# Linear sums over a whole group in 32-row tiles, paired 64-row transposes of x, no clip in the gate, and another written order

## The chip, the cores and the metric

The kernel runs on one core of a Trainium2 chip. The metric is the device time of one execution in microseconds, as the median of several runs. Before the change three runs took 248.51, 249.53 and 250.40 us, so the median is 249.53 us.

## What is computed

There are 4 batches of 12,480 rows x of width 128, and 32 inducing rows. Two attention steps follow one another, and a gated feed-forward layer stands behind them:

```python
def mab(q, kv):
    s = scale * (q @ kv.transpose(0, 2, 1))
    s = s - s.max(-1, keepdims=True)
    a = np.exp(s)
    a /= a.sum(-1, keepdims=True) + 1e-09
    return a @ kv
h = mab(I, x)          # 32 rows a batch
y = mab(x, h)          # 12480 rows a batch
g = y @ w_in                                   # 128 -> 2048
out = (g * np.clip(g + 3.0, 0.0, 6.0) / 6.0) @ w_out   # 2048 -> 128
```

Each row of y is a weighted mean of the 32 rows of h. While |g| stays below 3 the gate is the polynomial g(g+3)/6, so an output row is a linear sum over the 32 weights plus a quadratic sum over pairs of weights. The kernel computes h for a batch, multiplies its 32 rows through w_in, and folds w_out into two small matrices: one for the linear sums and one (four blocks of 128 pairs) for the quadratic sums. A test at the end counts entries that would leave the range of the approximation and branches to a plain version if there are any.

## The kernel before, in words

**Tiling.** A batch is cut into six groups of 2,048 rows and one of 192. Within a full group, partition p holds 16 consecutive rows. For the second attention these are seen as 4 slots s by 4 lanes j (J = 4, Sn = 4); a half h of a group is two slots.

**First attention, per group.** `op_X` loads x through GpSimd's queue, cast to fp16 on the way, into one of 7 buffers. `op_T` (line 422) transposes 8 or 16 blocks of 128x128 on TensorE into PSUM, `op_Y` (line 428) copies eight of them to xT. `op_S` forms scores, `op_E` the exponentials, `op_A` the sums over rows of x and `op_H` adds them to a batch's accumulator.

**Once a batch.** `op_c3` to `op_cN` turn the accumulator into the small matrices: `op_G` is the product with w_in, `op_cH` (line 543, GpSimd) and `op_cI` (line 548, VectorE) make g * min(max(g+3, 0), 6) from it, `op_L` multiplies by w_out, `op_cN` (line 595) writes the linear matrix BD, and `op_p`, `op_P`, `op_cX`, `op_cY` make the quadratic matrix Cq. `op_cJ` (line 553, VectorE) keeps the largest |g| for the test at the end. BD is written with a mask, so that each of its 64-row halves is a block-diagonal matrix for two lanes.

**Second attention and output, per group.** `op_Z` makes two score forms in PSUM; ScalarE and VectorE turn them into z, e, dk; `op_W` spreads dk over partitions with a DMA of 128 KB issued by SyncE's queue. For each half, `op_B` (line 731) repeats z over pairs into four PSUM banks and `op_F` (line 741, ScalarE, two instructions a half) takes the exponential into TF; `op_U` (line 750, VectorE) multiplies by the spread dk into TD. The sums are taken in PSUM: `op_l` (line 770) adds the linear part from ee and BD, `op_q` (line 789) the quadratic part from TF (u = 0) and TD (u = 1) with Cq. `op_v` multiplies a finished bank by the row's factor and writes it to os (line 807 on VectorE, line 811 on ScalarE in four pieces), and `op_O` stores os to memory from SyncE's queue.

A bank of the output sums holds one half h and one pair of lanes jp: two slots by two lanes by 128 columns. It gets two linear matmuls of 64 rows by 256 columns and 16 quadratic ones of 128 columns. A half needs two such banks; a full group uses four, two at a time or as the order has it.

**Order.** There is no scheduler. The string `ORDER` lists about 1,400 tokens such as `q.0.2.1.0.1.5`; each is one `op_` call, with batch, group, half and so on, the numbers of its PSUM banks (0 to 7) and, where there is a choice, the engine (V, A or P). Every engine executes its own instructions in the order of the string, and semaphores make an instruction wait for what it reads and for the buffer or bank that it overwrites. `op_w` issues matmuls on zeros, which only keep TensorE going while the first loads are under way.

Of the kernel before, what the change touches and what calls it, by code (L numbers as in the profile page):

```python
# [32 lines left out]
cD.0.0.V T.1.0.8.16.0 T.1.0.0.8.4 X.1.3.0.16 cH.0.P cD.0.1.A Y.1.0.8.16.0.V S.1.1.0.16.6 Y.1.0.0.8.4.A W.0.0.3
E.1.1.0.16.6 Z.0.3.0.5 Z.0.2.0.7 cI.0 Zz.0.2.7 p.0.2.V W.0.2.3 B.0.0.0.2.0 S.1.0.0.16.4 F.0.0.0.0.2 E.1.0.0.16.4 L.0.0.6
A.1.1.0.16.7 W.0.2.0 H.1.1.0.16.7 L.0.1.6 cL.0.6 p.0.1.V A.1.0.0.16.4 cM.0.0.6 W.0.1.0 Ze.0.0 cm.0.3 ee.0.0.V cN.0.3
cM.0.1.7 F.0.0.0.1.0 Ze.0.1 cC.0 wb.1.P T.1.3.8.16.2 H.1.0.0.16.4 R.0.0.0 wb.0.P Y.1.3.8.16.2.A p.0.3.V T.1.3.0.8.1
wb.2.P Rr.0.0.0 wb.3.P P.0.1.6 P.0.2.7 p.0.0.V Y.1.3.0.8.1.A R.0.1.4 Rr.0.1.4 R2.0.1.V X.1.2.0.16 B.0.0.1.2.0 Zz.0.3.5
F.0.0.1.1.0 P.0.3.7 F.0.0.1.0.2 cP.0.1.7 P.0.0.6 cP.0.0.6 W.0.1.3 W.0.1.2 B.0.1.0.4.0 F.0.1.0.0.4 Z.0.3.1.7 Zd.0.3.7
U.0.0.1 cX.0.0.3 S.1.3.0.16.2 cY.0.0.3.A F.0.1.0.1.0 T.1.2.8.16.6 T.1.2.0.8.4 Y.1.2.8.16.6.V E.1.3.0.16.2 cX.0.1.5
q.0.0.1.1.0.7 Ze.0.3 cY.0.1.5.V Y.1.2.0.8.4.V q.0.0.0.1.0.6 l.0.0.0.0.6 W.0.1.1 l.0.0.1.1.7 B.0.1.1.2.4 R2.0.0.V  # L40
q.0.0.0.0.0.0 q.0.0.1.1.1.7 U.0.0.0 q.0.0.0.0.1.0 v.0.0.1.1.7.V W.0.3.2 F.0.1.1.1.4 F.0.1.1.0.2 v.0.0.0.0.0.V
q.0.0.0.1.1.6 v.0.0.0.1.6.V q.0.0.1.0.0.1 q.0.0.1.0.1.1 B.0.2.0.2.4 R.0.3.0 v.0.0.1.0.1.V Ze.0.2 R.0.2.6 Rr.0.3.0
S.1.2.0.16.7 W.0.2.1 W.0.2.2 X.1.4.0.16 W.0.3.1 T.1.4.0.8.1 Rr.0.2.6 Y.1.4.0.8.1.V F.0.2.0.0.2 A.1.3.0.16.0 Z.0.4.1.6
W.0.3.0 X.1.5.0.16 X.2.4.0.16 W.0.3.3 Z.0.5.1.2 F.0.2.0.1.4 H.1.3.0.16.0 Z.0.4.0.3 Zd.0.4.6 E.1.2.0.16.7 B.0.2.1.0.4
# [986 lines left out]
```

## Time and profile before

| what | value |
|---|---|
| median of three runs | 249.53 us |
| the profiled execution, its own time | 249.51 us |
| its span, first to last instruction | 247.5 us |
| what lies outside the span | 2.0 us |
| TensorE busy, weight loads busy | 92%, 75% |
| VectorE, ScalarE, GpSimd busy | 82%, 77%, 16% |
| mean granted TensorE clock | 0.982 |

The profile's page gives the busy time of each engine, the same in 40 equal slices of the span, and groups of instructions by line. PE is TensorE's matmuls, PEld its weight loads, DVE is VectorE, ACT ScalarE, POOL GpSimd, SP SyncE. Matmuls are pipelined: one of 128 columns is listed at some 220 ns, while the next begins 56 ns after it. What a step takes is therefore read from where the next one starts in the timeline, not from its listed length. An idle time is given with what ended it. Times inside the program are counted from the start of the span.

### The profile page before, as it was taken

How to read it: one execution, taken by the hardware profiler on the slowest of the kernel's cores; microseconds unless marked ns; L12 is line 12 of the kernel's file. 1: busy time of each engine (PE TensorE's matmuls, PEld its weight loads, DVE VectorE, ACT ScalarE, POOL GpSimd, SP SyncE). 2: the span in 40 equal slices, each digit the busy share in tenths (PEclk: the TensorE clock that was granted, in tenths of full speed). 3: DMA queues.
4: the chain of work that ended last, by engine and by line, in shares of the span. 5: the costliest groups of instructions: out<-in, count | busy, mean ns of one | idle time of the engine just before them, and what ended most of it. 6: DMA issues, size and time to landing. Idle time of an engine off the chain costs nothing. (4 is left out here: it accounts for less than half of the span.)

```text
span 247.5 us, 10076 instructions
## 1 busy us (share of the span) xinstructions
PE 227.0 (92%) x4317; PEld 186.5 (75%) x4317; DVE 202.4 (82%) x438; ACT 191.1 (77%) x350; POOL 40.3 (16%) x80
## 2 busy tenths in 40 slices
PE   1879799999799999999899999999999999989990
PEld 0568758888698798797787888888878877768780
DVE  0236879989599997999778998988889999998983
ACT  2167277998788886999687786999889889989870
POOL 8518582021002500010004000000031000000000
PEclk9999679999999999999999999999999999999998
DMA  6999789969989999849879974623981849696953
GB/s 96 193 255 254 238 158 193 208 163 250 214 286 263 277 196 331 293 87 250 184 252 265 266 274 110 224 56 76 338 305 37 262 97 340 211 311 170 362 232 134
DMA packets 23744, 53.91 MB, mean 218 GB/s; under 512 B 3697, under 2 KB 16785, under 8 KB 20753
## 3 DMA queue, kind: packets, MB, share of 16 engines
q1 hardware_dynamic: 19072, 38.36, 47.4%
q0 software_dynamic: 4624, 14.88, 31.0%
q8 instruction: 34, 0.56, 0.8%
q14 instruction: 14, 0.11, 0.1%
HBM read 27.67 MB, written 25.56 MB: 215 GB/s over the span
## 5 line engine op out<-in xcount | busy, mean ns | idle before, releaser
L741 ACT ACTIVATE TF<-ps 128x1024 f16<-128x1024 f32 (+1 forms) x100 | 96.8, 1007 | 16.1 <-PE ps L731 12.4
L750 DVE TENSOR_TENSOR TD<-TF,d 128x2048 f16<-128x2048 f16 (+1 forms) x52 | 59.9, 1156 | 3.0 <-ACT TF L741 2.2
L789 PE MATMUL ps<-Cq,TF 128*128 128x128 f16 (+1 forms) x784 | 57.9, 219 | 2.6 <-issue 1.4
L789 PE MATMUL ps<-Cq,TD 128*128 128x128 f16 (+1 forms) x784 | 56.0, 219 | 0.0
L807 DVE TENSOR_TENSOR os<-ps,r 128x512 f32<-128x512 f32 x68 | 45.4, 683 | 11.7 <-PE ps L789 4.1
L789 PEld LDWEIGHTS <-TF 128*128 128x128 f16 (+1 forms) x784 | 46.3, 98 | 6.3 <-issue 6.0
L789 PEld LDWEIGHTS <-TD 128*128 128x128 f16 (+1 forms) x784 | 46.1, 99 | 4.3 <-issue 3.4
L811 ACT ACTIVATE os<-ps,r 128x128 f32<-128x128 f32 x112 | 32.0, 380 | 4.3 <-PE ps L789 2.0
L422 PE MATMUL ps<-ident_h,xh 128*128 128x128 f16 x384 | 29.8, 226 | 5.5 <-DMA xh<-in_x_dram 5.5
L422 PEld LDWEIGHTS <-xh 128*128 128x128 f16 x384 | 24.0, 102 | 11.6 <-DMA xh<-in_x_dram 7.5
L428 DVE COPY xT<-ps 128x1024 f16<-128x1024 f16 x31 | 21.2, 684 | 12.8 <-PE ps L422 12.5
L428 ACT COPY xT<-ps 128x1024 f16<-128x1024 f16 x17 | 17.0, 1015 | 18.9 <-PE ps L422 18.8
L416 POOL DMA_DIRECT2D xh<-in_x_dram x25 | 13.9, 560 | 75.1 <-PE ps L459 62.2
L731 PE MATMUL ps<-z,pair 32*128 32x256 f16 (+1 forms) x400 | 20.3, 270 | 0.0
L609 DVE TENSOR_TENSOR PR<-Gd 128x2048 bf16<-128x2048 bf16 x16 | 19.8, 1239 | 0.0
L678 DVE TENSOR_SCALAR_CACHE_REDUCE z<-ps 128x512 f16<-128x512 f32 (+1 forms) x28 | 17.3, 621 | 2.4 <-PE ps L656 2.3
L666 ACT ACTIVATE dk<-ps 128x512 f16<-128x512 f32 (+1 forms) x28 | 14.8, 547 | 5.5 <-PE ps L656 3.4
L770 PE MATMUL ps<-BD,ee 64*128 64x256 f16 (+1 forms) x196 | 17.5, 273 | 0.2
L441 ACT ACTIVATE a<-ps 128x512 f16<-128x512 f32 (+1 forms) x27 | 14.6, 556 | 2.6 <-PE ps L433 2.6
L616 PE MATMUL ps<-w_ob,PR 128*128 128x128 bf16 x256 | 16.5, 219 | 0.0
L671 ACT ACTIVATE e<-z 128x512 f16<-128x512 f16 (+1 forms) x28 | 16.3, 589 | 0.1
L616 PEld LDWEIGHTS <-PR 128*128 128x128 bf16 x256 | 14.7, 98 | 0.9 <-issue 0.8
(137 smaller groups left out, 284.8 us busy)
## 6 DMA issues: line engine op xcount, KB each, us to landing
out_dram<-os SPq DMA_DIRECT2D x23, 1024.0 KB, 5.2
d<-dk SPq DMA_DIRECT2D x96, 128.0 KB, 3.9
xh<-in_x_dram POOLq DMA_DIRECT2D x23, 512.0 KB, 8.8
os<-in_moe_w_in_dram POOLq DMA_DIRECT2D x2, 512.0 KB, 13.4
w_or<-in_moe_w_out_dram POOLq DMA_DIRECT2D x2, 512.0 KB, 11.6
out_dram<-os SPq DMA_DIRECT2D x2, 512.0 KB, 3.6
xh<-in_x_dram POOLq DMA_DIRECT2D x2, 256.0 KB, 7.3
out_dram<-osl SPq DMA_DIRECT2D x4, 96.0 KB, 3.0
```

What stands on the lines that cost most here:

```text
L422: nc.tensor.transpose(pt[:, (i - lo) * p : (i - lo + 1) * p], at(xh, xhl, b, g)[:p, i, :], ident_h[:p, :p])
L428: copier(e)(xT_of(b, g)[:, lo * p : hi * p], ps[:, k, :].bitcast(FP16)[:, : (hi - lo) * p])
L609: veng(e).tensor_mul(pr_of(b, c)[:, :, :].rearrange("p a (i m) -> p a i m", m=M), views[0], views[1])
L616: nc.tensor.matmul(ps[:, k, f * C : (f + 1) * C], lhsT=pr_of(b, c)[:, jb, :], rhs=w_ob[:, jb, :], start=first_of(b, u), stop=False, skip_g ...
L678: nc.vector.tensor_scalar(fat(z_, b, g)[:rows, :w], ps[:rows, k, :w], 1.0, None, op0=ALU.mult, op1=ALU.min, accum_out=z_all[:rows, b * NGR ...
L731: nc.tensor.matmul(ps[:, pairs[j // 2] + j % 2, f * w : (f + 1) * w], lhsT=pair[rows, f, :], rhs=fat(z_, b, g)[rows, h * w : (h + 1) * w], ...
L741: nc.scalar.activation(hat(TF_, b, g, h)[:, 2 * q : 2 * q + 2, :w], ps[:, k : k + 2, :w], ACT.Exp, scale=scale / KH)
L750: nc.vector.tensor_mul(split(hat(TD_, b, g, h)), split(hat(TF_, b, g, h)), d.unsqueeze(2).to_broadcast([P, J, 2, w]),)
L770: nc.tensor.matmul(ps[:p, ks[jp], s2 * 2 * C : (s2 + 1) * 2 * C], lhsT=fat(e2_, b, g)[rows, s * p : (s + 1) * p], rhs=BD_[b % 2][rows, :, ...
L789: nc.tensor.matmul(ps[:p, k, (s2 * 2 + j2) * C : (s2 * 2 + j2 + 1) * C], lhsT=t[:, j, f * w + s2 * p : f * w + (s2 + 1) * p], rhs=Cq_[b % ...
L807: nc.vector.tensor_mul(o, src, r.unsqueeze(3).to_broadcast([p, Sh, 2, C]))
L811: nc.scalar.mul(o[:, s2, j2, :], src[:, s2, j2, :], r[:, s2, j2 : j2 + 1])
```

## The change

- **Linear sums.** An output bank now holds one lane j with all four slots of a group (both halves). `op_l` runs once a group and issues 16 matmuls of 32 rows by 128 columns, four row tiles side by side, each into its own bank. BD is a plain 128x128 copy; the mask is gone. A bank gets 4 linear and 16 quadratic matmuls as before in number, but its quadratic ones come from both halves, so a group opens four banks together and `op_v` can empty one only behind the second half.
- **Transposes.** For batches 1 to 3, `op_TT` transposes a full group in 32 matmuls of 64 rows by 64 columns: two row tiles, one into each of two banks, for each of 16 blocks. `op_YY` copies one such bank to xT in 64-column pieces. x comes in two halves, X.b.g.0.8 and X.b.g.8.16, 36 loads in place of 18. Batch 0 and the groups of 192 rows keep `op_T` and `op_Y`, and batch 0 now loads group 0 whole as well.
- **No clip.** `op_cH` is gone; `op_cI` computes (g+3)*g at once. The test takes the sum of squares of g on ScalarE (`op_cJ`) against 9 in place of the largest |g| on VectorE against 3.
- **Stores.** `op_O` can store two lanes of a group; the last group is stored so.
- **Order.** All of ORDER is new. With it go these counts of instructions: `op_v` 74 on VectorE and 22 calls (88 pieces) on ScalarE, before 68 and 28 calls (112 pieces); copies to xT of 1,024 columns 23 on VectorE and 25 on ScalarE, before 31 and 17; matmuls on zeros 24, before 16; w_hi copies 1 on VectorE and 3 on ScalarE, before 3 and 1; w_lo 3 on VectorE, before 2; w_ob three of four on ScalarE, before all on GpSimd; the Gd copies 5 of 8 on ScalarE, before 4.

```diff
-it X.0.1.0.16 i2 i1 w.2.0 i3.V T.0.1.0.8.1 Y.0.1.0.8.1.V i0 w.2.5 w.2.2 X.0.0.8.16 T.0.0.8.16.1 w.2.7 Y.0.0.8.16.1.V
+i0 i2 w.2.4 w.2.2 w.2.7 wi.1 w.2.0 X.0.0.0.16 w.2.2 w.2.3 i1 i8 X.0.6.0.2 w.2.0 i3.V T.0.0.0.8.1 it Y.0.0.0.8.1.V
...
-        BD_ = ring("BD", 2, [P, 2, C], FP16)
+        BD_ = ring("BD", 2, [P, C], FP16)
...
+        def op_TT(b, g, *ks):
+            for i in range(TG):
+                for r in range(2):
+                    rows = slice(64 * r, 64 * r + 64)
+                    nc.tensor.transpose(
+                        ps[:, ks[r], :].bitcast(FP16)[:, i * 64 : (i + 1) * 64],
+                        at(xh, xhl, b, g)[rows, i, :],
+                        ident_h[rows, rows],
+                        tile_position=(64 * r, 0),
+                    )
+
+        def op_YY(b, g, r, k, e):
+            copier(e)(
+                xT_of(b, g)[:, :].rearrange("c (i r t) -> c r i t", r=2, t=64)[:, r],
+                ps[:, k, :].bitcast(FP16).rearrange("c (i t) -> c i t", t=64),
+            )
...
-        def op_cH(b, e):
-            veng(e).tensor_scalar(
-                r6[:, :, :], GL[:, :, :M].bitcast(FP32), 3.0, 0.0, op0=ALU.add, op1=ALU.max
-            )
-
         def op_cI(b):
             nc.vector.scalar_tensor_tensor(
-                GL[:, :, M:], r6[:, :, :], 6.0, GL[:, :, :M].bitcast(FP32), op0=ALU.min, op1=ALU.mult
+                GL[:, :, M:],
+                GL[:, :, :M].bitcast(FP32),
+                3.0,
+                GL[:, :, :M].bitcast(FP32),
+                op0=ALU.add,
+                op1=ALU.mult,
             )
 
         def op_cJ(b):
-            nc.vector.tensor_reduce(
-                g_all[:, b : b + 1],
+            nc.scalar.activation(
+                junk[:, :].rearrange("p (a m) -> p a m", m=M),
                 GL[:, :, :M].bitcast(FP32),
-                axis=AX.XY,
-                op=ALU.max,
-                apply_absolute_value=True,
+                ACT.Square,
+                accum_out=g_all[:, b : b + 1],
             )
...
-        def op_l(b, g, h, *ks):
-            t0, p, J, Sn = groups[g]
-            Sh = (Sn + 1) // 2
-            for s2 in range(Sh):
-                s = h * Sh + s2
-                for jp in range(J // 2):
-                    rows = slice(64 * jp, 64 * jp + 64)
+        def op_l(b, g, *ks):
+            t0, p, J, Sn = groups[g]
+            for s in range(Sn):
+                for j in range(J):
+                    rows = slice(32 * j, 32 * j + 32)
                     nc.tensor.matmul(
-                        ps[:p, ks[jp], s2 * 2 * C : (s2 + 1) * 2 * C],
+                        ps[:p, ks[0] + j if g == NG else ks[j], s * C : (s + 1) * C],
                         lhsT=fat(e2_, b, g)[rows, s * p : (s + 1) * p],
-                        rhs=BD_[b % 2][rows, :, :].rearrange("p j c -> p (j c)"),
+                        rhs=BD_[b % 2][rows, :],
-                        tile_position=(64 * jp, 0),
+                        tile_position=(32 * j, 0),
                     )
...
-                            ps[:p, k, (s2 * 2 + j2) * C : (s2 * 2 + j2 + 1) * C],
+                            ps[:p, ks[0] + j2 if g == NG else ks[j2], (h * Sh + s2) * C : (h * Sh + s2 + 1) * C],
```

**How the order moves, on VectorE near the end of batch 3.** The rows are instructions of VectorE in their order, with no time in them. TD<-TF,d is `op_U` of one half, os<-ps,r is `op_v`, r<-rc is the factor of a group, rc<-ps its reciprocal, ee<-e the square of e. Before, around the fourth and fifth groups of the batch:

```order
L717 RECIPROCAL rc_163<-ps 128x16
L807 TENSOR_TENSOR os_118<-ps,r_165 128x2x256
L723 TENSOR_TENSOR r_165<-rc_163 128x16
L692 TENSOR_TENSOR ee_100<-e_97 64x96
L723 TENSOR_TENSOR r_165<-rc_164 128x16
L750 TENSOR_TENSOR TD_115<-TF_112,d_110 128x2048
L807 TENSOR_TENSOR os_117<-ps,r_165 128x2x256
L750 TENSOR_TENSOR TD_116<-TF_113,d_111 128x2048
L807 TENSOR_TENSOR os_117<-ps,r_165 128x2x256 x3
L750 TENSOR_TENSOR TD_115<-TF_114,d_111 128x2048
```

The same place now:

```order
L812 TENSOR_TENSOR os_118<-ps,r_163 128x4x128 x4
L725 RECIPROCAL rc_161<-ps 128x16
L758 TENSOR_TENSOR TD_116<-TF_114,d_110 128x2048
L731 TENSOR_TENSOR r_163<-rc_162 128x16
L758 TENSOR_TENSOR TD_115<-TF_112,d_110 128x2048
L758 TENSOR_TENSOR TD_116<-TF_113,d_111 128x2048
L812 TENSOR_TENSOR os_117<-ps,r_163 128x4x128
L686 TENSOR_SCALAR z_103,z_all<-ps 64x96
L812 TENSOR_TENSOR os_117<-ps,r_163 128x4x128 x2
L758 TENSOR_TENSOR TD_115<-TF_114,d_111 128x2048
```

Before, a bank is emptied between the two products of a group; now both products (TF_114 and TF_112 with d_110) stand ahead of the first bank of that group (os_117).

**And at VectorE's end.** junk,cnt rows are the counts of the test; tot is the copy of their sum. Before:

```order
L807 TENSOR_TENSOR os_118<-ps,r_165 128x2x256 x2
L717 RECIPROCAL rc_164<-ps 96x2
L723 TENSOR_TENSOR r_165<-rc_164 96x2
L831 TENSOR_SCALAR junk,cnt<-g_all 128x4
L831 TENSOR_SCALAR junk,cnt<-d_all 128x128 x2
L831 TENSOR_SCALAR junk,cnt<-c_all 128x4 x2
L831 TENSOR_SCALAR junk,cnt<-h_all 128x4
L831 TENSOR_SCALAR junk,cnt<-z_all 128x28
L831 TENSOR_SCALAR junk,cnt<-r_165 128x98
L858 COPY tot<-ps 1x9
```

Now:

```order
L839 TENSOR_SCALAR junk,cnt<-z_all 128x28
L812 TENSOR_TENSOR os_118<-ps,r_163 128x4x128
L731 TENSOR_TENSOR r_163<-rc_162 96x2
L758 TENSOR_TENSOR TD_116<-TF_112,d_109 128x2x192
L812 TENSOR_TENSOR os_118<-ps,r_163 128x4x128
L812 TENSOR_TENSOR osl_120<-ps,r_163 96x256
L839 TENSOR_SCALAR junk,cnt<-r_163 128x98
L839 TENSOR_SCALAR junk,cnt<-r_163 128x294
L839 TENSOR_SCALAR junk,cnt<-g_all 128x4
L839 TENSOR_SCALAR junk,cnt<-d_all 128x128 x2
L839 TENSOR_SCALAR junk,cnt<-c_all 128x4 x2
L839 TENSOR_SCALAR junk,cnt<-h_all 128x4
L866 COPY tot<-ps 1x9
```

The count of z moved ahead of the last products, the count of 294 factors moved to the end, and the last output bank (osl) now stands on VectorE ahead of the counts.

More of the change, by code (lines that the diff above doesn't have):

```diff
@@ L153 @@
+O.3.6.0.2 y1 O.3.5.8.16 y0 y3 y4.3 y5.3
 """
@@ L351, in op_i6 @@
                 e.memset(blk[rows, j : j + 1], math.sqrt(KC))
-                e.memset(mask[rows, j % 2, :], 1.0)
             e.memset(fac[:, :], KC / 3.0)
@@ L594, in op_cN @@
         def op_cN(b, k):
[L595 to L597 removed]
+            nc.vector.tensor_copy(BD_[b % 2][:, :], ps[:, k, :C])
         def pr_of(b, c):
@@ L796, in op_q, with op_v @@
                         )
-        def op_v(b, g, h, jp, k, e):
+        def op_v(b, g, j, k, e):
             t0, p, J, Sn = groups[g]
-            Sh = (Sn + 1) // 2
-            o = at(os_, osl, b, g)[:p, : J * Sn, :].rearrange("p (s j) c -> p s j c", j=J)
-            o = o[:, h * Sh : (h + 1) * Sh, 2 * jp : 2 * jp + 2, :]
-            src = ps[:p, k, : Sh * 2 * C].rearrange("p (s j c) -> p s j c", j=2, c=C)
-            r = r2_of(b, g, 0, J * Sn).rearrange("p (s j) -> p s j", j=J)
-            r = r[:, h * Sh : (h + 1) * Sh, 2 * jp : 2 * jp + 2]
+            js = slice(0, J) if g == NG else slice(j, j + 1)
+            o = at(os_, osl, b, g)[:p, : J * Sn, :].rearrange("p (s j) c -> p j s c", j=J)[:, js]
+            src = ps[:p, k : k + js.stop - js.start, : Sn * C].rearrange("p j (s c) -> p j s c", c=C)
+            r = r2_of(b, g, 0, J * Sn).rearrange("p (s j) -> p j s", j=J)[:, js]
             if e == "V":
-                nc.vector.tensor_mul(o, src, r.unsqueeze(3).to_broadcast([p, Sh, 2, C]))
-            else:
-                for s2 in range(Sh):
-                    for j2 in range(2):
-                        nc.scalar.mul(o[:, s2, j2, :], src[:, s2, j2, :], r[:, s2, j2 : j2 + 1])
+                n = js.stop - js.start
+                nc.vector.tensor_mul(o, src, r.unsqueeze(3).to_broadcast([p, n, Sn, C]))
+            else:
+                for i in range(js.stop - js.start):
+                    for s in range(Sn):
+                        nc.scalar.mul(o[:, i, s, :], src[:, i, s, :], r[:, i, s : s + 1])
         def op_O(b, g, lo, hi):
@@ L816, in op_O @@
             r0 = b * N + t0
-            nc.sync.dma_start(
-                out[r0 : r0 + p * n, :].rearrange("(p i) c -> p i c", i=n)[:, lo:hi, :],
-                at(os_, osl, b, g)[:p, lo:hi, :],
-            )
+            o = out[r0 : r0 + p * n, :].rearrange("(p i) c -> p i c", i=n)
+            t = at(os_, osl, b, g)[:p]
+            if hi - lo == n:
+                nc.sync.dma_start(o, t)
+            else:
+                half = lambda a: a.rearrange("p (s j) c -> p s j c", j=J)[:, :, lo // 4 : hi // 4, :]
+                nc.sync.dma_start(half(o), half(t))
         def op_dr():
@@ L844, in op_y3 @@
         def op_y3():
-            count(3, g_all[:, :], 3.0, ALU.is_le)
+            count(3, g_all[:, :], 9.0, ALU.is_le)
             d = d_all[:, :, :].rearrange("p b m -> p (b m)")
```

277 lines of the change are left out of this document (134 added, 143 removed).

## The prediction

> **What bounds the kernel now.** I read the busy shares first, then the slices, then the windows.
>
> ```profile
> PE 227.0 (92%) x4317; PEld 186.5 (75%) x4317; DVE 202.4 (82%) x438; ACT 191.1 (77%) x350; POOL 40.3 (16%) x80
> ...
> PE   1879799999799999999899999999999999989990
> PEclk9999679999999999999999999999999999999998
> ```
>
> TensorE is the fullest engine, low only in the first slices and the last. Between, the windows say how full (busy us of PE, PEld, DVE, ACT, POOL in a stretch, then the granted clock):
>
> ```profile
> 28.00:40.00 12.00, 11.46 (x213) 8.88 (x213) 9.72 (x23) 8.27 (x14) 7.26 (x10) 0.76 0.80 170
> 28.00:241.00 213.00, 208.04 (x3977) 172.31 (x3976) 189.06 (x388) 178.61 (x330) 22.82 (x32) 0.99 0.78 221
> 200.00:220.00 20.00, 19.91 (x343) 15.86 (x340) 19.44 (x39) 19.23 (x37) 0.00 (x0) 1.00 0.78 245
> ```
>
> From 28 to 241 us PE idles 213.00 - 208.04 = 5.0 us. Its work sets the length of that stretch; a matmul removed there is time removed, until VectorE (89% of the stretch) or ScalarE (84%) is in the way. From 200 to 220 both stand at 96 to 97% and PE still works 19.91 of 20 us. Outside the stretch, the start waits for x and the end is a chain:
>
> ```profile
> 6.52 1.03 PE L422 MATMUL ps<-ident_h,xh 128*128 128x128 f16 x8 [4.28 <-DMA xh<-in_x_dram]
> ...
> 240.73 0.42 PE L789 MATMUL ps<-Cq,TD 128*96 128x128 f16 x4
> ...
> 243.10 0.20 PE L854 MATMUL ps<-cnt,ones 128*1 128x9 f32 x2 [1.95 <-DVE junk L831]
> ...
> 243.83 0.14 DVE L864 TENSOR_SCALAR bad_i<-cs 1x1 int32<-1x1 f32 x1
> ```
>
> What a step costs PE is read from start to start. This is the timeline of PE, then of its weight loads:
>
> ```profile
> 100.66 1.07 PE L789 MATMUL ps<-Cq,TF 128*128 128x128 f16 x16
> 101.56 1.06 PE L789 MATMUL ps<-Cq,TD 128*128 128x128 f16 x16
> 102.55 0.39 PE L770 MATMUL ps<-BD,ee 64*128 64x256 f16 x4
> 102.87 0.40 PE L731 MATMUL ps<-z,pair 32*128 32x256 f16 x8
> 103.20 0.62 PE L422 MATMUL ps<-ident_h,xh 128*128 128x128 f16 x8
> 103.66 0.55 PE L789 MATMUL ps<-Cq,TF 128*128 128x128 f16 x7
> ...
> 231.05 0.61 PE L770 MATMUL ps<-BD,ee 64*128 64x256 f16 x8
> 231.60 0.40 PE L731 MATMUL ps<-z,pair 32*128 32x256 f16 x8
> ```
>
> ```profile
> 102.55 0.11 PEld L770 LDWEIGHTS <-ee 64*128 64x128 f16 x4
> 102.87 0.12 PEld L731 LDWEIGHTS <-pair 32*128 32x128 f16 x8 [0.21 <-issue]
> ```
>
> Sixteen full matmuls of 128 columns take 101.56 - 100.66 = 0.90 us, 0.056 each. The next sixteen, with row tiles behind them, take 0.99: 0.09 more for the change of form. Four linear matmuls (two sets of two tiles, 256 columns) take 0.32, eight take 231.60 - 231.05 = 0.55; so a set costs 0.23 / 2 = 0.115 and leaving costs 0.32 - 0.23 = 0.09. Eight matmuls of op_B (two sets of four 32-row tiles, 256 columns) take 0.33, the same 0.115 a set: four tiles side by side cost what two cost. Eight transposes take 103.66 - 103.20 = 0.46, 0.0575 each.
>
> **The change part by part.**
>
> *Linear sums.* A group has 4 sets of 256 columns before and 4 sets of 128 columns now. A set of 128 should cost half of 0.115, 0.0575, or a little more for issuing four; I take 0.060. Per group 4 x (0.115 - 0.060) = 0.22 us, for 24 groups **-5.3 us**. Bounds: -5.5 with exactly half, 0 if a set of four tiles keeps the 0.115 of the nearest row, which had as many tiles.
>
> *Transposes.* 18 groups x 16 blocks = 288 blocks. Each cost 0.0575 in one matmul; now two of 64 columns in two row tiles. Side by side they take 0.115 x 64/256 = 0.029; one behind the other as long as one of 128 columns, 0.0575. I take 0.040, nearer the first, since all sets quoted ran side by side, with 0.011 for issuing twice as many. 288 x 0.0175 = **-5.0 us** (bounds -8.2 and 0).
>
> *Changes of form.* Counted in the two orders, 178 before and 187 now, as the paired transposes add a form of their own and the linear sums are called once a group: 9 x 0.09 = **+0.8 us**.
>
> So PE loses 9.5 us of work, bounds -12.9 to +0.8. The 8 further matmuls on zeros stand in the wait for the first x (4.28 us idle above); without that cover they cost a few tenths of a microsecond each.
>
> [...] In op_B eight weight loads of 32 rows ran within 0.12 us, four of them for row tiles whose matmuls were still streaming (0.33 us to the next step). [...]
>
> *VectorE and ScalarE.* The groups by line give busy time, then mean, of each kind:
>
> ```profile
> L811 ACT ACTIVATE os<-ps,r 128x128 f32<-128x128 f32 x112 | 32.0, 380 | 4.3 <-PE ps L789 2.0 <-PE ps L770 1.1 <-ACT e L671 1.0
> L807 DVE TENSOR_TENSOR os<-ps,r 128x512 f32<-128x512 f32 x68 | 45.4, 683 | 11.7 <-PE ps L789 4.1 <-DMA out_dram<-os 3.5 <-ACT TF L741 2.9
> L428 DVE COPY xT<-ps 128x1024 f16<-128x1024 f16 x31 | 21.2, 684 | 12.8 <-PE ps L422 12.5
> L428 ACT COPY xT<-ps 128x1024 f16<-128x1024 f16 x17 | 17.0, 1015 | 18.9 <-PE ps L422 18.8
> L609 DVE TENSOR_TENSOR PR<-Gd 128x2048 bf16<-128x2048 bf16 x16 | 19.8, 1239 | 0.0
> L543 POOL TENSOR_SCALAR r<-GL 128x512 f32<-128x512 f32 x4 | 8.6, 2143 | 7.1 <-DVE GL L532 4.1 <-DVE r L723 2.8 <-DVE hm L506 0.3
> L540 ACT CAST Gd<-GL 128x512 bf16<-128x512 f32 x4 | 2.4, 618 | 1.2 <-DVE GL L532 1.2
> L553 DVE TENSOR_REDUCE g_all<-GL 128x1 f32<-128x512 f32 x4 | 2.7, 665 | 0.0
> L641 ACT ACTIVATE junk<-Cp 128x512 f32<-128x512 f16 x4 | 2.5, 635 | 0.0
> L641 ACT ACTIVATION_READ_ACCUMULATOR junk<-Cp 128x1 f32 x4 | 0.8, 201 | 0.0
> L402 ACT CAST w_hi<-os 128x512 bf16<-128x512 f32 x1 | 1.1, 1130 | 0.0
> L402 DVE CAST w_hi<-os 128x512 bf16<-128x512 f32 x3 | 2.1, 723 | 0.7 <-DMA os<-in_moe_w_in_dram 0.7
> ```
>
> ScalarE, by busy time over count: 24 pieces of op_v less, 24 x 0.286 = -6.9; 8 copies to xT more, +8.0; the squares of g, priced as those of Cp, (2.5 + 0.8) = +3.3; one Gd copy more +0.6; two w_hi copies +2.2; three w_ob copies priced as a Gd copy, +1.9. Sum **+9.1**, to about 200 us. VectorE: 6 op_v more, 6 x 45.4/68 = +4.0; 8 copies less, -5.5; the reduction of g -2.7; two w_hi copies less -1.4; one w_lo and other small ones about +0.5. Sum **-5.1**, to about 197 us. The 64-column pieces of op_YY I price as plain copies, since PR, written from 32-element pieces, keeps 1239 ns for 2048. At ScalarE's price per element (1015 for 1024) they would cost VectorE 16 x 0.33 = 5.3 us more, and it would stay at 202.
>
> None of this is on PE's path by itself, but three engines now lie within 20 us of each other. In a stretch of 204 us PE has 198.5 us of work, ScalarE some 186 (91%), VectorE some 184 (90%). With every output bank open until the group's second half is done, PE has also fewer free banks to run ahead in. I charge **+3.0 us** for added waiting: less than PE's present 5.0, because at 96 to 97% of both engines PE still ran 19.91 of 20. Bounds 0 and, with 0.3 us a group, 7.
>
> *No clip.* op_cH was 2.1 us on GpSimd between op_cG and op_cI, four times. PE had other work there (11.46 of 12.00 busy at 28 to 40 us), so I cost its removal at nothing. If that work were not there, up to 2.1 us in the first batch would be gained. The start otherwise depends on the same loads: w_in's second half now leads the queue and its first half follows, so equally much stands ahead of batch 0's last x. Bounds for the start -2 and +2, because the clock was 0.76 at 28 to 40 us and either order can lose or regain it.
>
> *Loads in halves.* 18 more issues on GpSimd, which is 16% busy; hidden, unless both halves of a group, for which op_TT waits, come late.
>
> *The end.*
>
> ```profile
> L831 DVE TENSOR_SCALAR_CACHE_REDUCE junk<-r 128x294 f32<-128x294 f32 x1 | 0.5, 460 | 0.0
> L807 DVE TENSOR_TENSOR osl<-ps,r 96x256 f32<-96x256 f32 x2 | 0.8, 416 | 0.1
> L723 DVE TENSOR_TENSOR r<-rc 96x2 f32<-96x2 f32 x4 | 0.6, 149 | 0.0
> L717 DVE RECIPROCAL rc<-ps 96x2 f32<-96x2 f32 x4 | 0.7, 163 | 0.0
> ```
>
> From the last quadratic sums to the matmul of the counts it was 243.10 - 240.73 = 2.4 us. Now the last linear sum (about 0.3 with its changes of form), op_v of osl (0.42) and the count of 294 factors (0.46 + 0.08) stand there, while reciprocal, factor (0.31) and the count of z (about 0.26) went ahead: **+0.7 us**.
>
> *Sum*, against the profiled execution's own 249.51 us (the median is 249.53): 249.5 - 9.5 + 3.0 + 0.7 = **243.7 us**.
>
> **The rivals.**
>
> *A, all of it comes.* Transposes at 0.029, no added waiting, 1 us regained at the start: 249.5 - 5.3 - 8.2 + 0.8 + 0.7 - 1 = 236.5 us; I give it everything below 240. For it: 96% on two engines left PE at 19.91 of 20. Against: batch 0 and the small groups don't change, and ScalarE gets 9 us more.
>
> *B, ScalarE and the banks take it back.* ScalarE idled 213.0 - 178.6 = 34.4 us in the long stretch. To end 9 us sooner with 7 us more work that idle time must shrink to 18. If it only shrinks to 26, the stretch is 186 + 26 = 212 and the whole about 249 us. For it: op_F's two instructions stand between the two halves of each group; against: the stretch at 96%.
>
> *C, slower: a group's four banks stop PE.* The place is op_q behind op_U of the second half. Before, half the banks could be emptied while the second half was made; now the next group's first sum needs banks that only the last op_v frees, while op_B needs four more of the eight. From 0.36 us a group (8.8 us, which is 9.5 - 0.7, over 24) the change gains nothing. With one op_v on VectorE (0.67) waited for in each group it is 24 x 0.67 = 16.0: 249.5 - 9.5 + 0.7 + 16.0 = 256.7 us. For it: order on VectorE, where both products now stand ahead of a group's first op_v. Against: the tokens put other groups' op_B, op_S and transposes between.
>
> [...]
>
> **How the numbers follow.** Forecast (240 to 247) 0.60, A 0.14, B (247 to 252) 0.15, C 0.09, D 0.02. A measurement of this kernel can tell about 1%, 2.5 us, from no change: faster by more is 0.60 + 0.14 = 0.74, within 0.15, slower 0.11. The range, 238 to 250.5 us, takes in the upper half of A and most of B; it leaves about 0.2 outside.
>
> **What would show it.** Right: a paired transpose of 16 blocks takes 0.6 to 0.7 us between its start and the end of its last set, a group's linear sums 0.24 us beside the changes of form, ScalarE stands near 200 us, and PE is busy over 95% of the long stretch. Wrong in the transposes: 0.9 us or more for 16 blocks. Wrong in the waiting: PE idle over 9 us between 28 us and its last sums, with op_v or op_F as releaser. Wrong as a whole: a time above 250.5 us, or below 238.

## The result, and the profile after

The change made the kernel slower: 259.03 us (257.11 to 260.23, 4 runs) against 249.02 (247.51 to 250.40, 4 runs) of the kernel before on the same chip, a ratio of 1.040 with a 95% interval of 1.030 to 1.049. The forecast was 243.7. Ratios here and below leave disturbed runs (over 1.5% above the fastest of their kernel) out and medians do not, so where the two differ the ratio counts; only e6's ratio is made of disturbed runs (its two others took 256.92 and 260.09 us), and the profiles of e9, e13 and e14 are of such runs. The profiled execution took 260.23 us, its span 258.9.

The page of the changed kernel: busy time by engine, then the span in 40 slices for TensorE and its granted clock.

```profile
PE 226.8 (88%) x4809; PEld 186.4 (72%) x4809; DVE 196.9 (76%) x431; ACT 198.2 (77%) x349; POOL 34.1 (13%) x82
...
PE   8699779779996799999946999999989999999970
...
PEclk9979979979999799999995999999999999999995
```

VectorE and ScalarE stand where they were forecast (197 and 200). TensorE's row has holes near slices 8, 13 and 21 that it did not have before, and each is followed by a low clock. The windows give the long stretch (PE, PEld, DVE, ACT, POOL busy, granted clock, DMA share, GB/s):

```profile
28.00:250.00 222.00, 204.04 (x4456) 170.48 (x4457) 183.64 (x383) 183.78 (x326) 17.11 (x35) 0.96 0.76 212
200.00:220.00 20.00, 19.99 (x371) 16.83 (x368) 17.88 (x33) 18.65 (x39) 0.00 (x0) 1.00 0.64 207
```

PE idles 222.00 - 204.04 = 18.0 us, where it idled 5.0 before. Of this, 15.6 us lie between 28 and 145 us (3.1 before), where the DMA engines are busiest: their share there was 0.90 before and is 0.85 now, behind it 0.65 and 0.66. Late in the program, from 200 to 220 us, PE is as full as ever: the loss is not there. The timeline of PE (start, listed length) prices the new steps:

```profile
129.54 0.40 PE L776 MATMUL ps<-BD,ee 32*128 32x128 f16 x16
129.78 0.39 PE L739 MATMUL ps<-z,pair 32*128 32x256 f16 x8
...
149.09 1.14 PE L428 MATMUL ps<-ident_h,xh 64*128 64x64 f16 x64
150.16 0.40 PE L776 MATMUL ps<-BD,ee 32*128 32x128 f16 x16
```

A group's linear sums take 129.78 - 129.54 = 0.24 us beside the changes of form, as forecast. The 32 blocks of two groups take 150.16 - 149.09 = 1.07 us with one change of form of 0.09, so 0.98 / 32 = 0.031 a block, less than the 0.040 forecast. TensorE's work did shrink.

What grew is waiting. These are the stops of more than 3 us, from the timelines around them; the bracket holds the idle time before an instruction and what ended it:

```profile
52.69 1.22 DVE L758 TENSOR_TENSOR TD<-TF,d 128x2048 f16<-128x2048 f16 x1 [3.55 <-DMA d<-dk]
52.81 0.60 ACT L674 ACTIVATE dk<-ps 128x512 f16<-128x512 f32 x1 [3.48 <-DMA d<-dk]
53.46 0.64 PE L428 MATMUL ps<-ident_h,xh 64*128 64x64 f16 x32 [3.26 <-ACT dk L674]
...
84.50 1.14 ACT L816 ACTIVATE os<-ps,r 128x128 f32<-128x128 f32 x4 [3.95 <-DMA out_dram<-os]
85.69 0.62 PE L664 MATMUL ps<-xT,Wd 128*32 128x512 f16 x4 [3.38 <-ACT os L816]
...
136.17 1.23 DVE L758 TENSOR_TENSOR TD<-TF,d 128x2048 f16<-128x2048 f16 x1 [6.14 <-DMA d<-dk]
138.05 0.59 PE L444 MATMUL ps<-I_T,xT 128*128 128x32 f16 x16 [5.52 <-DVE os L812]
```

Read each from the bottom up. (Where the text gives the length of a stop without a bracket, it counts from the start of the last matmul before it to the start of the next, some 0.2 us more.) TensorE waits for a bank that ScalarE or VectorE empties; that engine stands in its own order behind an instruction that waits for a transfer: at 52.7 and 136.2 us a spread of dk (128 KB), at 84.5 us the store of an earlier group, whose tile the next products need. From issue to landing these took 9.9 us (42.74 to 52.66), 9.5 us (74.93 to 84.42) and 8.9 us (127.08 to 135.95). Of the spreads in general the page's transfers say (KB each, median us from issue to landing), before the change

```profile
out_dram<-os SPq DMA_DIRECT2D x23, 1024.0 KB, 5.2
d<-dk SPq DMA_DIRECT2D x96, 128.0 KB, 3.9
xh<-in_x_dram POOLq DMA_DIRECT2D x23, 512.0 KB, 8.8
```

and after it

```profile
out_dram<-os SPq DMA_DIRECT2D x23, 1024.0 KB, 5.6
d<-dk SPq DMA_DIRECT2D x96, 128.0 KB, 4.3
xh<-in_x_dram POOLq DMA_DIRECT2D x36, 256.0 KB, 9.0
```

Medians moved little. The three transfers above were issued among x loads: seven half loads between 39.4 and 42.6 us, two near 74 us, two at 126.6 and 127.1 us. They are not the only late ones: 16 of the 104 spreads took over 8 us, up to 11.8, where before the change 8 did, up to 11.3. Most of these stop nothing; what counts is also how soon the product comes that needs them (see below).

Each stop is paid twice. The windows around two of them:

```profile
51.40:54.80 3.40, 1.34 (x46) 1.29 (x46) 2.11 (x3) 1.99 (x4) 0.00 (x0) 1.00 1.14 209
54.80:58.20 3.40, 3.40 (x50) 2.79 (x48) 1.56 (x3) 2.36 (x5) 0.00 (x0) 0.50 0.93 174
...
133.30:136.70 3.40, 0.00 (x0) 0.00 (x0) 0.53 (x1) 0.00 (x0) 1.54 (x3) 1.00 1.03 388
136.70:143.50 6.80, 5.44 (x84) 4.54 (x84) 4.83 (x18) 3.25 (x5) 0.00 (x0) 0.50 0.96 195
```

While PE stands still the DMA engines are full (share 1.14 and 1.03; it adds up the times of the packets, so it can pass 1), and for the next 3.4 or 6.8 us PE is granted half its clock. Matmuls then take about twice as long: 16 blocks of paired transposes from 36.48 to 37.45 us, in another such window, took 0.97 us in place of 16 x 0.031 = 0.50.

**The sum, from the traces.** The long stretch grew from 213 to 222 us, by 9.0. Of this +13.0 is idle time (18.0 for 5.0) and +4.8 half clock: there PE worked 15.5 us at half clock (34.33 to 37.74, 54.81 to 58.22, 85.53 to 88.94 and 136.73 to 143.55 us), before 5.9 us (28.00 to 33.85), and half of such time is lost, by the 0.97 us for 0.50 above. What remains is the work, 9.0 - 13.0 - 4.8 = -8.8 us, for -9.5 forecast. Behind the stretch 1.7 us more came (the end, below): 249.5 + 9.0 + 1.7 = 260.2 us, beside 260.23 measured.

### The profile page after: what moved, and what is told of

Its sections match the earlier page's. It is cut to its first block, busy times and chain, and to the rows that moved or that the text cites. A ratio compares the mean times of both kernels' runs of the same rounds, so it can differ in the third digit from the quotient of the medians.

```text
span 258.9 us, 11047 instructions
## 1 busy us (share of the span) xinstructions
PE 226.8 (88%) x4809; PEld 186.4 (72%) x4809; DVE 196.9 (76%) x431; ACT 198.2 (77%) x349; POOL 34.1 (13%) x82
## 3 DMA queue, kind: packets, MB, share of 16 engines
q1 hardware_dynamic: 19840, 38.36, 45.5%
q0 software_dynamic: 7072, 14.88, 30.6%
## 4 chain that ended last, share of the span: by engine, by line
PE 61%; DMA 15%; DVE 7%; ACT 6%; SPq 3%; issue 3%; POOL 1%; DVEq 0%; ACTq 0%; POOLq 0%
PE ps L795 29%; DMA d<-dk 8%; PE ps L739 5%; PE ps L624 4%; PE ps L664 4%; DMA xh<-in_x_dram 4%; DMA out_dram<-os 4%; PE ps L444 3%; ACT TF L749 3%; SPq L706 3%; PE ps L460 3%; PE ps L428 3%; DVE os L812 2%; PE ps L776 2%; PE ps L416 2%
## 5 line engine op out<-in xcount | busy, mean ns | idle before, releaser
L758 DVE TENSOR_TENSOR TD<-TF,d 128x2048 f16<-128x2048 f16 (+1 forms) x52 | 59.1, 1147 | 14.7 <-DMA d<-dk 10.4
L795 PE MATMUL ps<-Cq,TD 128*128 128x128 f16 (+1 forms) x784 | 57.6, 222 | 0.9 <-issue 0.4
L812 DVE TENSOR_TENSOR os<-ps,r 128x512 f32<-128x512 f32 x74 | 48.5, 684 | 10.9 <-PE ps L795 7.3
L410 POOL DMA_DIRECT2D xh<-in_x_dram x42 | 22.6, 548 | 82.3 <-PE ps L470 62.7
L816 ACT ACTIVATE os<-ps,r 128x128 f32<-128x128 f32 x88 | 24.8, 385 | 4.4 <-DMA out_dram<-os 3.9
L739 PE MATMUL ps<-z,pair 32*128 32x256 f16 (+1 forms) x400 | 22.0, 275 | 0.9 <-ACT TF L749 0.4
L436 ACT COPY xT<-ps 128x1024 f16<-128x1024 f16 x20 | 19.6, 1021 | 2.3 <-PE ps L428 2.1
L444 PE MATMUL ps<-I_T,xT 128*128 128x32 f16 x384 | 13.9, 178 | 6.6 <-DVE os L812 5.5
L444 PEld LDWEIGHTS <-xT 128*128 128x128 f16 x384 | 12.3, 97 | 8.8 <-issue 7.1
L428 PE MATMUL ps<-ident_h,xh 64*128 64x64 f16 x576 | 12.0, 196 | 4.9 <-ACT dk L674 3.3
L428 PEld LDWEIGHTS <-xh 64*128 64x128 f16 x576 | 10.2, 98 | 7.1 <-issue 6.5
```

The source lines that it names most:

```text
L410: nc.gpsimd.dma_start(at(xh, xhl, b, g)[:p, lo:hi, :], src[:, lo:hi, :])
L428: nc.tensor.transpose(ps[:, ks[r], :].bitcast(FP16)[:, i * 64 : (i + 1) * 64], at(xh, xhl, b, g)[rows, i, :], ident_h[rows, rows], tile_po ...
L436: copier(e)(xT_of(b, g)[:, :].rearrange("c (i r t) -> c r i t", r=2, t=64)[:, r], ps[:, k, :].bitcast(FP16).rearrange("c (i t) -> c i t", ...
L444: nc.tensor.matmul(ps[:p, k, i * M : (i + 1) * M], lhsT=xT_of(b, g)[:, i * p : (i + 1) * p], rhs=I_T[:, :],)
L739: nc.tensor.matmul(ps[:, pairs[j // 2] + j % 2, f * w : (f + 1) * w], lhsT=pair[rows, f, :], rhs=fat(z_, b, g)[rows, h * w : (h + 1) * w], ...
L758: nc.vector.tensor_mul(split(hat(TD_, b, g, h)), split(hat(TF_, b, g, h)), d.unsqueeze(2).to_broadcast([P, J, 2, w]),)
```

## The experiments

Theory: *late transfers*. The work went nearly as forecast, but single transfers land some 9 us after their issue, the engines behind them stop, and the clock falls. The first rival was C of the prediction, *the four open banks of a group stop PE*. When the first runs had answered that, the rivals became three forms of the theory: the **halves** (more and smaller pieces), the **sequence** on SyncE's queue, and the **traffic** as a whole.

| run | us, median | ratio to before, 95% interval |
|---|---|---|
| changed kernel | 259.03 | 1.040 [1.030, 1.049] |
| e1 after, 36 of 46 x loads left out | 242.82 | 0.976 [0.970, 0.983] |
| e2 before, 19 of 29 x loads left out | 246.75 | 0.991 [0.987, 0.994] |
| e3 after, spreads of group 0.0 first | 256.33 | 1.024 [1.016, 1.032] |
| e4 after, full transposes | 259.72 | 1.040 [1.029, 1.051] |
| e5 before, loads in halves | 252.19 | 1.017 [1.005, 1.029] |
| e6 after, whole loads | 261.57 | 1.055 [1.046, 1.064] |
| e7 after, spreads early | 339.90 | 1.373 [1.359, 1.388] |
| e8 after, spreads and stores early | 257.19 | 1.035 [1.026, 1.044] |
| e9 after, eight half loads left out | 251.25 | 1.003 [0.997, 1.009] |
| e10 after, stores early | 332.47 | 1.335 [1.323, 1.347] |
| e11 after, four edits of order | 333.88 | 1.341 [1.330, 1.352] |
| e12 after, queue by ready time | 254.82 | 1.018 [1.008, 1.028] |
| e13 after, half of each store left out | 250.83 | 1.003 [0.998, 1.008] |
| e14 after, third store tile | 259.57 | 1.037 [1.024, 1.049] |
| e15 e12 with the third tile | 252.71 | 1.017 [1.005, 1.028] |
| e16 e15, one half load moved | 255.48 | none on record |
| e17 e15 with whole loads | 252.54 | 1.011 [1.007, 1.015] |

### e1 and e2: x loads left out

```diff
-X.1.3.8.16 X.1.3.0.8 ... X.3.6.0.2
+                       # batches 1 to 3, but for the first uses of a buffer
```

> The changed kernel without 36 of its 46 loads of x: batches 1 to 3 work on what batch 0 and the first groups of batch 1 left in the buffers, so the output is not the reference's; all other work stays. Theory 'late transfers': the three stops of TensorE (3.4, 3.4 and 5.7 us) end when a spread of dk or a store lands 9 to 10 us after its issue, because loads of x stand among them; without these loads the stops and the slow clock behind them (about 6 us) go, and the time falls by 15 to 20 us to 239 to 244 us. Rival 'four banks': TensorE waits because a group's four banks stay open; the time stays above 250 us.

> The kernel before without 19 of its 29 loads of x, in the same way (output not the reference's). Theory 'late transfers': it had few such stops, so it falls by 1 to 4 us, to 245 to 248 us; the difference between the two kernels without loads is then the saved work of TensorE, 4 to 9 us in favour of the changed one. Rival 'four banks': the changed one stays slower here too.

The changed kernel fell by 16 us, the kernel before by 2. The windows and the waits of e1, where nearly all of TensorE's work and every bank are as in the changed kernel:

```profile
28.00:233.00 205.00, 199.79 (x4455) 167.51 (x4456) 183.59 (x383) 183.28 (x326) 1.74 (x5) 0.98 0.58 185
```

```profile
DVE TD L755 <- DMA d<-dk: 1.1, 1, 1.1
```

Idle time is back at 5.2 us, and VectorE waits for spreads 1.1 us in all, where in the changed kernel it waited 10.4:

```profile
DVE TD L758 <- DMA d<-dk: 10.4, 4, 6.1
```

So the open banks cost nothing that can be seen: rival C is out. Without x traffic the change is worth 246.75 - 242.82 = 3.9 us. In the long stretch it is 5 us (205.0 us, for 210.0 of e2 from 28 to 238 us): 8.4 us less work (8.8 above), against which e1 has 1.6 us more idle time and 1.7 us more half clock. The rest is lost behind the stretch. The x loads stand on GpSimd's queue, and yet it is SyncE's spreads that land sooner without them (3.94 us on the mean, for 5.00), so loads on one queue delay transfers of the other.

### e3 and e4: one stop mended, and the transposes undone

```diff
-W.0.1.1 ... W.0.1.2 ... W.0.1.0 ... W.0.0.1 ... W.0.1.3 ... W.0.0.3 ... W.0.0.0 ... W.0.0.2
+W.0.0.1 ... W.0.0.3 ... W.0.0.0 ... W.0.0.2 ... W.0.1.1 ... W.0.1.2 ... W.0.1.0 ... W.0.1.3
```

> The changed kernel with one change of order: the four spreads of batch 0's group 0 are issued ahead of those of group 1, in the same eight places of the order. Theory 'late transfers': the stop at 50.0 us (3.4 us) and the half clock behind it (1.7 us) go; 253 to 256 us, unless other spreads come late in their place. Rival 'four banks': no change, 257 to 260 us.

```diff
-TT.1.0.5.3 ... YY.1.0.0.5.A
+T.1.0.0.8.5 T.1.0.8.16.3 ... Y.1.0.0.8.5.A
```

> The changed kernel with the 18 groups' paired transposes put back to full 128x128 ones, at the same places of the order and into the same two banks; loads stay in halves. TensorE's work grows by 288 x (0.0575 - 0.031) = 7.6 us less 13 visits' changes of form (2.5 us), about +5 us. If TensorE's work still sets the time between the stops: 262 to 266 us. If the transfers alone set it: 258 to 260 us.

By the ratios (1.024 for 1.040) e3 came down some 4 us, as the theory expected, though the intervals still overlap a little: the stop near 50 us is gone, but one of 2.0 us stands at 37 and one of 2.5 at 87 us, and that of group 1.3 has grown to 6.3 us. e4 gave TensorE its 5 us of transposes back and ended where the changed kernel did. The windows say where they went:

```profile
28.00:249.00 221.00, 206.26 (x4164) 175.52 (x4162) 183.04 (x383) 183.87 (x325) 17.25 (x34) 0.98 0.76 213
```

PE idles 14.7 us for 18.0 and worked 9.7 us at half clock for 15.5: more work, less waiting, the same end. By the same sum as above the work is 5.1 us more, so the paired transposes were worth that with all their changes of form. While the transfers set the time, the transposes were free here.

### e5 and e6: halves alone, and halves undone

```diff
-X.1.1.0.16
+X.1.1.0.8 X.1.1.8.16
```

> The kernel before with its 18 whole loads of x of the batches 1 to 3 cut in two halves, one right behind the other on GpSimd's queue; nothing else is changed, the transposes stay those of before. By the theory of late transfers in the form 'the halves do it' (twice the descriptors, smaller pieces, so that a small transfer between them lands later) most of the loss is here: 254 to 258 us, and spreads of the exponentials that land 4.9 to 5.2 us after their issue instead of 4.45. By the same theory in the form 'the order does it' (spreads and stores stand closer to their users than before, whatever the loads look like) the time stays at 248.5 to 251 us.

> The changed kernel with each pair of half loads put back into one whole load, at the place of the half that comes first; all else is the changed kernel, its 64-row transposes too. If the halves do it: back to 244 to 250 us and the stops of TensorE near 50, 82 and 132 us under 1 us each. If the order does it: 256 to 260 us, with at least two of the three stops still there and ended by a spread or by a store.

Halving alone cost the kernel before 1.7%, some 3.6 us at the medians, between the two forecasts. These are the transfers of GpSimd's queue (x loads and weights: packets, MB, share of the DMA engines' span), before and in e5:

```profile
q0 software_dynamic: 4624, 14.88, 31.0%
q0 software_dynamic: 7216, 14.88, 33.4%
```

33.4% of a span of 248.6 us for 31.0% of 247.5 is 6.3 us more for the same bytes; in the changed kernel it is 2.5 us more (30.6% of 258.9). Putting the halves together in the changed kernel did not bring the 244 to 250 us of the first forecast (e6): its two fastest runs took 256.92 and 260.09 us, and two of its three stops stayed, ended as before. The halves are a small cost, not the cause.

### e7, e8, e10 and e11: the sequence on SyncE's queue

Spreads (W) and stores (O) share one queue, and it works in order: one that is not ready holds all behind it, as the waits below show (VectorE 82.9 us for stores in e7, 61.3 us for spreads in e10). e7 moves each W to right behind its exponential, e10 each O to right behind its last product, e8 does both; e11 is e10 with the edit of e3 and two smaller moves.

```diff
-Zd.1.3.7 W.1.3.3 ... O.1.0.0.16 ... W.1.3.0 ... W.1.3.2 ... W.1.3.1
+Zd.1.3.7 W.1.3.3 W.1.3.0 W.1.3.2 W.1.3.1
```

> The changed kernel with each of the 104 spreads (d from dk) taken from its place and put right behind the exponential it copies (or behind the last product that frees its buffer, where that comes later in the order); on SyncE's queue they then also stand ahead of stores that they stood behind. If spreads issued too near their users are the cause: the stops near 50 and 132 us shrink by 2 us or more each, with them the slow clock behind them, and the time comes to 249 to 254 us; the stop near 82 us, ended by a store, stays. If it is the halves, whose traffic delays a transfer whenever it is issued: 256 to 259 us, since the same bytes then run beside the same loads a little earlier.

> As the run with early spreads, and each store of a finished group put right behind the last product that fills it (in the changed kernel the store stands 25 to 128 steps of the order further back, the first store of the second group 62). If spreads and stores issued too late are the whole cause: all three stops shrink, and the time comes to 243 to 249 us, the forecast of the work alone. If the halves do it, or if stores issued early only run into the loads: 252 to 258 us.

> The changed kernel with each store of a finished group right behind the last product that fills it, and nothing else moved: the second store can then go out near 68 us, when its last product is done, instead of 74.9 us, where it stood behind spreads that waited. By 'the queue order makes single transfers late': the stop near 82 us goes with its slow window, the two others stay, 251 to 256 us. By 'too many bytes all the way': 256 to 260 us, with a stop of like size elsewhere.

> All edits of order that aim at the three stops at once: the spreads of group 0.0 ahead of those of 0.1, each store right behind its last product, the four spreads of group 1.3 together behind their exponential, and the first half load of 3.4 behind those of 3.5. No instruction is added or taken away. By 'the queue order makes single transfers late': 243 to 249 us. By 'too many bytes all the way': 254 to 259 us, the stops only moving.

No expectation came near 332 and 340 us. The waits of e7 (in all, times, longest):

```profile
DVE os L812 <- DMA out_dram<-os: 82.9, 15, 10.3
ACT os L816 <- DMA out_dram<-os: 45.4, 9, 9.7
```

and of e10:

```profile
DVE TD L758 <- DMA d<-dk: 61.3, 13, 9.8
```

With spreads ahead, finished stores stand behind spreads that are not ready; with stores ahead, ready spreads stand behind stores whose products are not done. From each transfer's ready time (its exponential done and its buffer free, or its last product done) to its issue, on the mean: a spread waits 4.3 us before the change, 3.8 after it, 10.9 in e10; a store 4.0, 7.0 and, in e7, 16.2. e11 took over e10's stores and with them its loss, so it told nothing on its other edits. e8, where both waits are short (2.0 and 0.6 us), still took 257 us: it has a stop of 5.5 us at 79 us for the same store of group 0.1, which was ready at 69.6 us and went out at 74.6 behind the spreads of group 0.5, and one of 3.8 us at 141 us for a load of x.

### e9 and e13: bytes taken away

```diff
-X.2.2.0.8 X.2.2.8.16 X.2.1.8.16 X.2.1.0.8 X.2.5.0.8 X.2.3.0.8 X.3.4.0.8 X.3.3.8.16
```

> The changed kernel without eight of its 36 half loads of x: the four of the groups 2.1 and 2.2, which are in flight at the stop near 50 us, the first halves of 2.3 and 2.5 (near 82 us) and the half loads of 3.4 and 3.3 that go out at 126.6 and 127.1 us. What is left out is x for these rows; every other instruction stays, the transposes too. By 'three collisions': the three stops and the slow clock behind each go (12.5 us and some 6.8 us), so 240 to 246 us, nearly what leaving out 36 loads gave. By 'too many bytes all the way': eight halves are 22% of the halves, so about a fifth of the 16 us that leaving out all gave: 254 to 257 us.

```diff
-O.0.0.0.16
+O.0.0.0.8
```

> The changed kernel with only the first half of each store (half of the tile of 22 full groups is not written; the last group is stored whole as before). 11.5 MB less go over the DMA engines, all of it on SyncE's queue; all x loads stay. If the traffic as such delays the spreads: 242 to 249 us, like the run without x loads, which took 9 MB away. If it is the loads of x in particular (many small pieces on GpSimd's queue): 255 to 260 us. If it is the sequence on SyncE's queue alone: 252 to 258 us, since a store still waits and blocks as before, though it lands sooner.

Both came level with the kernel before, about 9 us under the changed one. In e9 the stops near 82 and 132 us are gone and the first has shrunk to 1.7 us (the longest left between 28 and 240 us is 1.9 us). e9 fell between its two forecasts: eight half loads, 22%, brought over half of what leaving out 36 brought, so place matters; but not all of it, so the traffic elsewhere costs too. In e13 (23 stores halved, 12.1 MB less) the stores landed in 4.1 us and the spreads in 3.7 (median), with all x loads in place:

```profile
q1 hardware_dynamic: 28672, 26.30, 37.2%
...
out_dram<-os SPq DMA_DIRECT2D x25, 512.0 KB, 4.1
d<-dk SPq DMA_DIRECT2D x96, 128.0 KB, 3.7
```

So it is not x in particular: bytes of either kind delay the spreads (at the median 4.3 us in the changed kernel, 3.8 in e1, 3.7 here). Nor does the number of pieces decide here: SyncE's queue carried 28,672 packets, more than the changed kernel's 19,840, and the time still fell. The stop at 129 us stayed, with 3.9 us, ended by a spread of group 1.3.

### e12, e14, e15, e16 and e17: mending it

e12 puts SyncE's transfers in the sequence of the ready times that the trace shows. e14 gives stores a third tile (NOS = 3, for one tile of xT; a score pass of group 0.2 and its exponential stand earlier to make this safe), e15 does both, e16 and e17 add one edit to e15.

```diff
-NXT = 13
-NOS = 2
+NXT = 12
+NOS = 3
```

> The changed kernel with the 104 spreads and 29 stores put on SyncE's queue in the sequence of the times at which the profile of the changed kernel shows each to be ready (its exponential done and its buffer free; the last product of its group done); every other engine's order is as in the changed kernel. In the changed kernel a spread goes out 3.8 us and a store 7.0 us after it is ready, on the mean; this takes nearly all of that away. If the sequence on the queue is the cause: 243 to 249 us. If the traffic is: 253 to 259 us, with stops of 3 us and more in new places, ended by spreads, stores or loads that took 8 us or more from their issue.

> The changed kernel with a third tile for finished groups, so that the products of a group wait for the store three groups back, not two. Its room (8 KB a partition) comes from one of the 13 tiles of transposed x (4 KB) and from what was free; to make that safe the pass Z of group 0.2 and its exponential stand some 40 steps earlier. All else is the changed kernel. By 'single collisions': the stop near 82 us (3.65 us and a slow window of 3.41 us) goes, the stops near 50 and 132 us stay: 252 to 256 us. By 'traffic as a whole': 256 to 260 us, with another stop in its place.

> The sequence on SyncE's queue by ready times and the third tile together. By 'single collisions': the stop of 6.3 us near 77 us of the run by ready times goes with its two slow windows (6.8 us at half clock), 244 to 249 us. By 'traffic as a whole': 251 to 256 us.

> As the run before, with the first half load of x of group 3.4 (whose transposes come last of all) behind the two of 3.5, for whose landing TensorE stopped near 140 us in the run by ready times. By 'single collisions': one to three us less than the run before, 242 to 248 us. By 'traffic as a whole': no difference to it, within its interval.

> The run with the sequence by ready times and the third tile, with each pair of half loads of x put together at the place of the first of them. If the halves are a cost of their own, as in the kernel before, where they cost 3.6 us: 248 to 250 us. If the changed order needs its data in halves (a whole load lands later for the transposes that wait) or the halves cost nothing here: 252 to 256 us.

e12 gained 2.2% (1.018 for 1.040), some 5 us, and kept one long stop, once more for that store:

```profile
82.48 1.14 ACT L816 ACTIVATE os<-ps,r 128x128 f32<-128x128 f32 x4 [6.77 <-DMA out_dram<-os]
83.67 0.62 PE L664 MATMUL ps<-xT,Wd 128*32 128x512 f16 x4 [6.08 <-ACT os L816]
```

The third tile alone (e14) took the stop at 82 us away and gained nothing; the spreads' stops stayed and two of 2.2 and 2.1 us came. With the sequence (e15) it is 2 us better by the medians and no better by the ratios (1.017 for 1.018), so its worth is not shown. The windows of e15:

```profile
28.00:240.00 212.00, 200.14 (x4453) 167.79 (x4454) 183.78 (x383) 183.18 (x325) 17.36 (x35) 0.98 0.79 222
```

PE idles 11.9 us there, less than the changed kernel's 18.0 but more than the 5.2 of e1; no wait for a spread or a store is left among its larger waits, and its longest stop, 2.3 us, ends with a load of x. e16's runs scatter from 251.9 to 259.0 and decide nothing. In e17 whole loads may be worth another microsecond (1.011 for 1.017); the intervals overlap. Mended, the changed kernel gains 2 to 3%, some 5 to 7 us, and none beats the kernel before. What stays open: whether any order of these steps carries all the traffic without stops, and why the mended kernel stays some 10 us above e1; 6.7 us of that is idle time. An order of the x loads themselves was not tried beyond e16. The linear sums and the missing clip were not run by themselves.

## Why the prediction was wrong

**What held.** Linear sums -5.3: 0.24 us a group, as forecast. Transposes -5.0: a block took 0.031 in place of 0.040, which alone would be 288 x 0.0265 = -7.6, but e4 shows 5.1 us in all. The 2.5 us between them are changes of form by the estimate made ahead of e4, which no run shows alone; so this term came out in part by luck. The work as a whole was -8.8 for -9.5. ScalarE 198.2 for "about 200", VectorE 196.9 for "about 197". D, at 0.02, asked for small sets that cost far more than forecast; at 0.24 us a group and 0.031 a block it is out. The end, from the last quadratic sums to the matmul of the counts, was +0.8 for +0.7:

```profile
249.98 0.39 PE L795 MATMUL ps<-Cq,TD 128*96 128x128 f16 x4
...
250.30 0.26 PE L776 MATMUL ps<-BD,ee 32*96 32x128 f16 x2
...
253.20 0.20 PE L862 MATMUL ps<-cnt,ones 128*1 128x9 f32 x2 [2.65 <-DVE junk L839]
```

253.20 - 249.98 = 3.2 us, where it was 2.4. From the matmul of the counts to the end of the execution 7.0 us passed, for 6.4; the forecast had no term for that.

**The step that failed** is "I charge +3.0 us for added waiting ... Bounds 0 and, with 0.3 us a group, 7". Idle time grew by 13.0 us, and half clock in the long stretch, which had no term of its own, took 4.8, together +17.8. The term was sized from engines (how full ScalarE and VectorE stood at 200 to 220 us), and that stage was indeed harmless, at 19.99 of 20 us. But the order had been rewritten for the stage from 28 to 145 us too, where x loads, spreads and stores together fill the DMA engines (share 0.90 before, 0.85 after), and there no landing time was looked at. "hidden, unless both halves of a group, for which op_TT waits, come late" was wrong in what it asked: GpSimd's issues were hidden, but the pieces cost time on the DMA engines (e5). The trace of before had the warning. From the landing of a group's last spread to the product that uses it there were 4.1 us (median of 28 groups). The spreads of group 0.1 took 8.9 to 11.3 us and stopped nothing, as the last landed at 49.8 us and its product began at 54.7. In the new order the median is 2.3 us, and at 8 of 28 groups it is 0.4 or less (at one before). Comparing the two orders along SyncE's queue would have shown that group 0.0's spreads now stand behind 0.1's (they were ready at 31.5 us and went out from 38.8 to 42.7 us), and that the store of group 0.1 stands behind a spread of 0.5 (2.8 us from ready to issue, 0.1 before). That a spread waits for its issue is not new (4.3 us on the mean before, 3.8 now): the slack behind it is what went.

**The rivals.** C's 256.7 us came near for another reason. It priced one op_v for each group's banks; what was seen is three places, each with a DMA as the last releaser, gone in e1 with the banks as they were. B, ScalarE's idle time, did not decide: 222.0 - 183.8 = 38 us of it were left. A had the price of a transposed block nearly right (0.029 for 0.031), but neither the work (-12.7 with its terms, for -8.8) nor the time. **No clip** at nothing was not tested alone.

**"What would show it"** named an idle time of over 9 us "with op_v or op_F as releaser". The idle time came, and op_v stood in the bracket at two of the stops; followed one step further back, it was a transfer. A releaser that is itself late is not the cause.

## What to carry to other kernels

When a change rewrites the order of a kernel whose DMA engines are nearly full over a stage, list for each transfer its ready, issue and landing time and the slack to its first user, before and after, and count only work that such slack covers as gained. A queue that works in order needs its transfers in the sequence in which they become ready: moving only one kind forward cost 73 to 81 us here. A stop of TensorE can cost more than its length: the three of over 3 us in the changed kernel were each followed by 3.4 or 6.8 us at half clock, so price that with it.

## What the runs showed of the hardware

**Half clock after short stops.** In the changed kernel a stop of 1.77 us (32.59 to 34.36), for which the profile shows no releaser, was already followed by half clock:

```profile
30.90:34.30 3.40, 1.73 (x57) 1.37 (x57) 2.01 (x6) 2.41 (x7) 0.00 (x0) 1.00 1.12 337
34.30:37.70 3.40, 3.34 (x80) 2.30 (x81) 2.01 (x6) 2.03 (x3) 0.61 (x1) 0.50 0.48 113
```

All stretches of half clock in the changed kernel begin on one grid of 3.41 us: those at 13.85, 34.33, 54.81, 85.53 and 136.73 us stand 6, 6, 9 and 15 such steps apart, and one at 252.78 us, in the end of the program, 34 more. The trace has two clocks only, 1.00 and 0.50. All began from full clock; the windows of the grid ahead of them held 1.65, 1.73, 1.35, 0.19, 0.00 and 1.18 us of work in 3.41. No sharp limit shows: before the change a window with 2.15 us of work (23.61 to 27.02 us) was followed by half clock, in the changed kernel one with 2.11 us (7.02 to 10.44 us) by full clock. What decides is open.

**Among x loads a small transfer took as long as a large one.** In the changed kernel a spread of 128 KB took 4.3 us at the median, and 9.9 and 8.9 us at two of the stops, issued among x loads (DMA share 1.09 and 1.02 from issue to landing); a store of 1 MB took 5.6 us at the median and 9.5 at the third (DMA share 0.94).
